# Two transformer layers on one core: all eight PSUM banks become one pool

## The chip, the core and the metric

The program runs on one core of a Trainium2 chip. The core has a tensor engine (TensorE, PE in the profile; its weight loads are the row PEld), a scalar engine (ScalarE, ACT), a vector engine (VectorE, DVE), GpSimd (POOL) and a queue that starts transfers (SyncE, SP). Each engine works through its own list of instructions in order and waits on semaphores for the others. Matmuls write into PSUM, here an array of 8 banks of 512 float32 values in each of 128 partitions; ScalarE and VectorE read them from there. The metric is the device time in microseconds (us); smaller is better.

## The reference

The input is 2048 tokens by 512 features. Four blocks run one after the other, each added to its input: attention, a mixer with an MLP, attention again, a mixer with an MLP again. The weights are the same both times.

```
def _A_ref(x, wq, wk, wv, wo):                 # x is the layer norm of the input
    q = (x @ wq).reshape(B, S, H, Dh)          # 32 heads of 16, one shared k and v
    k = x @ wk
    v = x @ wv
    scores = jnp.einsum("bhqd,bkd->bhqk", q, k) * (Dh ** -0.5)
    p = _softmax(scores, axis=-1)
    o = jnp.einsum("bhqk,bkd->bhqd", p, v)
    return o.reshape(B, S, H * Dh) @ wo

def _B_ref(x, w1, w2, w3, w4):
    h = _gelu(_layernorm(x) @ w1)              # then shift its four quarters by +-1, +-2 tokens
    x1 = x + shifted(h) @ w2
    return x1 + _gelu(_layernorm(x1) @ w3) @ w4
```

With 32 heads of only 16 features over 2048 keys, most of the work is the scores' exponentials: 32 x 2048 x 2048 of them in each layer.

## The kernel before, in words

**Tiling.** A layer's queries are cut into chunks (`CHUNKS`, line 539 on): four of 512 tokens in layer 0, three of 512 and two of 256 in layer 1. In a chunk, a block is four heads, and there are eight blocks. A block goes over 16 tiles of 128 keys, in two halves of two heads each. One such half is a *unit* of scores: for 512 queries a matmul of 32 rows for each of two heads into a bank of 512 values each (`qk`, line 1083). There are 2048 units. In the chunks of 256 queries a unit takes two key tiles at once. Chunk 0 of layer 1 is worked on while layer 0's last work still delivers keys; its blocks are cut into segments whose sums are spilled and taken up again (`make_groups`).

**Two ways for a unit.** `declare_unit` (line 1111) sends a unit to ScalarE: two banks of scores, then one exponential over both (line 1127) into one of eight buffers EA. `declare_pair` (line 1133) sends a unit to VectorE instead: each head's scores go to one bank, VectorE turns them into the bits of a coarse exponential (line 1145), and a shift by integer addition (line 1182, GpSimd, or VectorE where GpSimd has much to do) makes the two further terms that refine it. Such a unit has three terms against one in the product with the values. `assign` decides how many units go this way: it is asked when a unit's score matmuls are placed (`attach`) and looks at the free banks, VectorE's queue and the pairs in flight.

**Values.** `declare_pv` (line 1232) multiplies each term by the values and the ones beside them, 256 columns in four column tiles, and adds them up in the accumulator bank. `block_end` evicts the accumulator with VectorE (lines 1244, 1250, 1264 or 1268), sends the sums by DMA to OT, and has the softmax's denominators gathered, inverted and multiplied in.

**Side work.** Projections, mixer, MLP and norms of finished chunks run in between: their matmuls (line 676, in halves that share a bank) take a bank and VectorE evicts it. All matmuls of this kind, and filler matmuls of zeros (`filler`) that keep the tensor engine active, are placed where the attention leaves room.

**Banks.** Banks 0 to 3 belong to ScalarE's units, which take pairs 0-1 and 2-3 in turn. Bank 4 is the accumulator of every block, one after the other. Banks 5, 6 and 7 are a pool: a `Late` object stands for a bank that is chosen when the first matmul into it is placed (`take`) and goes back when its reader has been placed (`give`).

```
ACT_SLOTS = (0, 2)
ACC = 4
POOL_BANKS = (5, 6, 7)
```

When the last unit has been placed, `pump` lends the other five banks to the pool (`lend`).

**Order.** `Plan` is a planner that runs while the program is built. It steps through time with a cost for every operation and puts each engine's instructions into a fixed order. `_pick` (line 204) chooses for an engine among the operations that are ready: by priority (scores of units 0, scores of VectorE's halves 0.5, values 2, second halves of projections CLOSE, side work 10), with exceptions. For the tensor engine it knows that a change between the scores' row tiles ("Q") and the others' column tiles ("P") costs SWITCH; VectorE's scores wait for a run of scores that is going anyway (`deferred`); side work must end before the next unit's scores are due (`limits`, `due`). `TEMPER` holds a letter for each 12.5 us of planned time; it picks one of sixteen settings (`MOODS`) of nine of the planner's rules.

## Time and profile before

| | |
|---|---|
| median of 3 runs | 1471.91 us (1471.07 to 1472.3) |
| profiled execution | 1472.13 us |
| its span | 1470.2 us |
| granted clock of TensorE | 1.00 |
| TensorE busy | 1446.2 us, 98% |
| ScalarE busy | 1406.4 us, 96% |
| VectorE busy | 1295.5 us, 88% |
| GpSimd busy | 1140.3 us, 78% |
| units on ScalarE / on VectorE | 1406 / 642 |
| HBM traffic | 7.90 MB read, 2.10 MB written |

The times come from one profiled execution. A group's row gives line, engine, operation, output and input by name and shape, its count, then its busy time and the mean of one in nanoseconds, then the idle time of the engine just before, and what ended it. A row of waits gives the waiting engine and line, what it waited for, the total in us, how many times, and the longest. Ends of matmuls are modelled, so that a busy tensor engine may still be waiting inside. In the chain that ended last each piece is a start, a length and what ran.

### The profile page before, as it was taken

The page shows a single profiled execution, that of the slowest core. Times are in us where ns is not written, and L with a number is a line of the kernel's source. Part 1 is how long each engine was busy: PE and PEld are TensorE (multiplying, and loading weights), DVE is VectorE, ACT ScalarE, POOL GpSimd, SP SyncE. Part 2 cuts the span into 40 slices and gives each one's busy share as a digit, 9 for nine tenths or more (in the row PEclk, how much of TensorE's full clock was granted, in tenths as well). Part 3 has the DMA queues.
Part 4 walks back from the last instruction along what each step waited for, and adds up shares of the span by engine and source line. Part 5 has one row for each costly group of instructions (what it writes and reads, how often), then busy time and mean ns, then how long its engine had stood idle before and what let it go on. Part 6 is the DMA issues. An engine that isn't in the chain of part 4 may idle for free.

```text
span 1470.2 us, 65395 instructions
## 1 busy us (share of the span) xinstructions
PE 1446.2 (98%) x29813; PEld 646.8 (44%) x29813; DVE 1295.5 (88%) x2323; ACT 1406.4 (96%) x1496; POOL 1140.3 (78%) x830
## 2 busy tenths in 40 slices
PE   9999999999999999999999999999999999999999
PEld 4344334444443444444444444444433344555565
DVE  8899999989999889998987899999989998889873
ACT  7999999999999999999979999999999999999962
POOL 2888887878898778899854789789769968788951
PEclk9999999999999999999999999999999999999999
DMA  6100100001000000100000000010000000000000
GB/s 217 31 6 6 20 5 7 6 5 20 6 6 5 6 4 6 21 6 2 3 3 3 3 10 10 6 21 5 9 18 8 4 6 8 20 15 7 8 15 24
DMA packets 32662, 21.76 MB, mean 15 GB/s; under 512 B 13056, under 2 KB 31872, under 8 KB 32384
## 3 DMA queue, kind: packets, MB, share of 16 engines
q1 hardware_dynamic: 32384, 17.57, 5.2%
q8 instruction: 233, 3.82, 1.1%
q14 instruction: 45, 0.37, 0.1%
HBM read 7.90 MB, written 2.10 MB: 7 GB/s over the span
## 4 chain that ended last, share of the span: by engine, by line
ACT 73%; PE 22%; DVE 3%; POOL 2%; issue 0%; POOLq 0%
ACT EA L1127 68%; PE PB L676 8%; PE PB L1083 6%; PE PB L1232 6%; ACT G L1615 2%; POOL J L1182 1%; ACT L1127 1%; DVE J L1145 1%; ACT GP L1535 1%; PE PB L876 1%; ACT L1535 1%; ACT L1615 1%; DVE G L1610 0%; PE PB L933 0%; DVE J L1182 0%
## 5 line engine op out<-in xcount | busy, mean ns | idle before, releaser
L1127 ACT ACTIVATE EA<-PB 128x1024 bf16<-128x1024 f32 x1406 | 1292.9, 1172 | 12.3 <-PE PB L1083 6.1
L1182 POOL TENSOR_SCALAR J<-J 128x2048 uint16<-128x2048 uint16 (+1 forms) x534 | 976.6, 1829 | 213.9 <-DVE J L1182 90.1
L1145 DVE TENSOR_SCALAR J<-PB 128x512 uint16<-128x512 f32 x1284 | 821.8, 681 | 81.6 <-PE PB L1083 77.5
L1083 PE MATMUL PB<-QT,KT 32*128 32x512 bf16 (+1 forms) x4608 | 603.0, 360 | 11.7 <-ACT EA L1127 5.0
L1232 PE MATMUL PB<-J,VD 128*32 128x256 bf16 (+1 forms) x8628 | 418.5, 265 | 3.0 <-POOL J L1182 1.1
L1232 PE MATMUL PB<-EA,VP 128*32 128x256 bf16 (+1 forms) x6340 | 343.8, 263 | 1.0 <-DVE QT L1244 0.3
L1083 PEld LDWEIGHTS PB<-QT,KT 32*128 32x128 bf16 x4608 | 162.6, 91 | 383.6 <-ACT EA L1127 313.1
L1232 PEld LDWEIGHTS PB<-J,VD 128*32 128x32 bf16 x8628 | 179.0, 95 | 180.5 <-issue 131.1
L1232 PEld LDWEIGHTS PB<-EA,VP 128*32 128x32 bf16 x6340 | 147.6, 95 | 111.1 <-issue 91.0
L676 PE MATMUL PB<-ZT,W 128*32 128x512 bf16 (+2 forms) x2816 | 168.7, 342 | 0.6 <-DVE ZT L885 0.3
L1182 DVE TENSOR_SCALAR J<-J 128x2048 uint16<-128x2048 uint16 (+1 forms) x136 | 98.6, 725 | 7.2 <-POOL J L1182 6.5
L676 PE MATMUL PB<-W,G 128*32 128x512 bf16 x1624 | 103.5, 380 | 0.0
L1610 DVE CAST G<-PB 128x512 bf16<-128x512 f32 (+2 forms) x126 | 72.2, 581 | 11.4 <-PE PB L676 8.7
L676 PEld LDWEIGHTS PB<-ZT,W 128*32 128x32 bf16 x2816 | 63.8, 96 | 33.4 <-issue 19.3
L812 POOL TENSOR_TENSOR SM<-SM,MH 128x2 f32<-128x2 f32 (+1 forms) x69 | 50.7, 735 | 22.0 <-DVE SM L814 13.3
L1615 ACT ACTIVATE G<-G 128x1792 bf16<-128x1792 bf16 x29 | 47.0, 1686 | 19.5 <-DVE G L1610 19.4
L676 PEld LDWEIGHTS PB<-W,G 128*32 128x32 bf16 x1624 | 38.0, 96 | 37.8 <-issue 11.0
L676 PE MATMUL PB<-ONES,NIL 128*32 128x512 bf16 x532 | 49.2, 407 | 1.4 <-DVE ZT L885 0.4
L792 DVE BATCH_NORM_STATS2 ST<-X 128x6 f32<-128x512 bf16 x64 | 42.9, 678 | 1.6 <-DMA X<-in_A_x_dram 1.3
L1591 POOL TENSOR_TENSOR X<-Y,X 128x512 bf16<-128x512 bf16 x32 | 39.0, 1225 | 6.8 <-DVE Y L1573 5.9
L1268 DVE CAST ACCF<-PB 128x512 bf16<-128x512 f32 (+1 forms) x65 | 40.1, 616 | 3.7 <-PE PB L1232 3.4
L814 POOL TENSOR_SCALAR SM<-MV 128x2 f32<-128x2 f32 (+1 forms) x45 | 12.3, 272 | 31.6 <-DVE MV L794 29.7
(108 smaller groups left out, 767.3 us busy)
## 6 DMA issues: line engine op xcount, KB each, us to landing
OT<-ACCF SPq DMA_DIRECT2D x432, 8.0 KB, 1.8
W<-in_B_w_dram SPq DMA_DIRECT2D x2, 1792.0 KB, 15.0
X<-in_A_x_dram SPq DMA_DIRECT2D x8, 256.0 KB, 5.0
QT<-QS SPq DMA_DIRECT2D x32, 64.0 KB, 2.4
out_dram<-OUTB SPq DMA_DIRECT2D x16, 128.0 KB, 1.7
OT<-ACCF SPq DMA_DIRECT2D x112, 4.0 KB, 2.2
W<-in_B_w_dram SPq DMA_DIRECT2D x2, 512.0 KB, 9.8
WQ<-in_A_wq_dram SPq DMA_DIRECT2D x1, 512.0 KB, 4.6
```

The costliest lines, as they stand in the source:

```text
L676: ins = e.matmul(self.PB[32 * g:32 * g + 32, bank, 0:n], lhsT=lhsT[:, 32 * g:32 * g + 32], rhs=rhs, start=start, stop=stop, tile_position= ...
L792: op("DVE", lambda e, tb=tb: e.bn_stats(self.ST6[:, tb, :], src(tb)), reads=[tagf(tb)], writes=[("ST", tb)], dur=0.606, prio=prio)
L812: op("POOL", lambda e: e.tensor_tensor(out=out, in0=src, in1=self.MH[:, 0, a:b], op=ALU.pow), reads=tags + [("MH",)], writes=tg(r), dur=0. ...
L1083: ins = e.matmul(self.PB[:, bank, j * n:(j + 1) * n], lhsT=self.KT[32 * h:32 * h + 32, la, (kb + j) * 128:(kb + j + 1) * 128], rhs=self.QT ...
L1127: o = q.feeds = op("ACT", lambda e: e.activation(self.EA[:, ea, :, :], self.PB[:, b0:b0 + 2, :], ACTF.Exp, scale=0.25), writes=bk + [("EA" ...
L1145: o = op("DVE", lambda e, i=i, L=L: e.tensor_scalar(out=self.J[:, 3 * s, i * 512:(i + 1) * 512], in0=self.PB[:, L.bank, :], scalar1=128 * ...
L1182: o = self.pl.op(eng, lambda e: e.tensor_scalar(out=self.J[:, d, :], in0=self.J[:, f, :], scalar1=float(self.STEP), scalar2=1.0, op0=ALU.a ...
L1232: ins = e.matmul(self.PB[32 * x:32 * x + 32, self.ACC, p * hw:p * hw + hw], lhsT=v[:, la, kb + j, :], rhs=ap[:, i, j * w + u * hw:j * w + ...
L1268: self.last_copy = op("DVE", lambda e: e.tensor_copy(acc, self.PB[:, self.ACC, 0:n]), writes=[("AC",)] + am, dur=t_ps(n), prio=0, side=False)
L1591: op("POOL", lambda e, tb=tb: e.tensor_tensor(out=self.X[:, tb, :], in0=self.Y[:, tb % 6, :], in1=self.X[:, tb, :], op=ALU.add), reads=[(" ...
L1610: op("DVE", lambda e, f=f, L=L: e.tensor_copy(self.G2[:, f, 0:n], self.PB[:, L.bank, 0:n]), writes=[L] + [(x, f, i) for x in ("G2", "GE") ...
L1615: op("ACT", lambda e, i=i: e.activation(self.G2[:, :, i * 128:(i + 1) * 128], self.G2[:, :, i * 128:(i + 1) * 128], ACTF.Gelu_apprx_tanh), ...
```

## The change

Every bank is in the pool. A unit for ScalarE takes two neighbouring banks when its score matmuls are placed, and gives them back after its exponential. An accumulator is a bank of the pool too, taken at a block's first value matmul and given back at the eviction, so that the next block can begin in another bank.

Who may take what is decided in `_pick`. `coming` lists the units whose exponentials are next, with the latest start of their score matmuls (`d`), the time from which a couple of neighbours is free for them (`at`), and whether they are urgent (within LEAD and the change of mode of `d`). A unit that is not urgent is placed only where a run of scores is going and LEFT banks remain (JOIN is its priority then). `couple` picks two neighbours, 0-1 or 2-3 before others. `single` picks one bank, 4 to 7 before others, and refuses one that would leave the next unit without a couple by its time, if that is within HORIZON; units, value matmuls and fillers are not refused. `limits`, `due` and `lend` go.

Beside this, a pair for VectorE may be started with one free bank at hand (FREE 1 for 2), CLOSE is 1.9 for 2.5 and so lies below the values' priority of 2, the planner's cost of the denominators' matmuls is 60 columns for 100, the tensor engine's first matmul (which cleared bank 4) goes, and TEMPER has other letters. Other evictions are changed like the one that is shown.

```diff
-    CLOSE = 2.5
+    CLOSE = 1.9
...
+    LEAD = 0.4
+    JOIN = 0.7
+    LEFT = 1
+    HORIZON = 1.0
...
-        limit = self.limits(t) if eng == "PE" and not dense else ()
+        coming = self.coming(t) if eng == "PE" and h else ()
+        limit = [max(d, at) + self.SLACK for q, d, at, urgent in coming[:1] if at < 1e8] if not dense else ()
         joins = eng == "PE" and t < self.pe_end - 1e-9
         low = self.deferred(h, t, joins) if eng == "PE" and not dense else {}
-        pressing = joins and any(o.prio == 0 and o.ready <= t + 1e-9 for o in h) and self.pe_kind != "Q"
+        pressing = joins and self.pe_kind != "Q" and any(urgent and at <= t + 1e-9 for q, d, at, urgent in coming)
+        nfree = sum(1 for x, b in self.pool if x + self.LAT["PE"] <= t + 1e-9)
+        by = None
+        if coming and not self.loose and coming[0][1] < t + self.HORIZON and coming[0][2] < 1e8:
+            by = max(coming[0][1], t)
         stick = eng == "PE" and not dense and not joins and self.STICK is not None and t < self.pe_end + 0.05 \
             and self.pe_kind == "P" \
             and not any((0 < o.prio <= self.RUSHED if o.side else self.closing) and o.ready <= t + 1e-9 for o in h)
-        due = list(limit) + self.due(h, t) if stick else ()
+        due = limit if stick else ()
...
+            if o.feeds is not None:
+                urgent = next((x[3] for x in coming if x[0] is o), None)
+                if urgent is None:
+                    continue
+                if not urgent:
+                    if not (self.pe_kind == "Q" and t < self.pe_end + 0.05) or nfree - 2 < self.LEFT:
+                        continue
+                    key = (self.JOIN, o.seq)
...
-                k = sorted(i for i in range(len(self.pool)) if self.pool[i][0] + margin <= t + 1e-9)
-                k = sorted(sorted(k, key=lambda i: self.pool[i][0])[:o.take.n])
-                if len(k) < o.take.n or o.prio > 2 and len(self.pool) <= self.SPARE and self.attach is not None and not self.loose:
+                k = self.couple(t, margin) if o.take.n > 1 else \
+                    self.single(t, margin, None if o.feeds is not None or o.prio in (2, -20) else by)
+                if k is None:
...
+    def free_banks(self):
+        f = [1e9] * 8
+        for x, b in self.pool:
+            f[b] = x
+        return f
+    def single(self, t, margin, by):
+        f = self.free_banks()
+        best = None
+        for b in range(8):
+            if f[b] + margin <= t + 1e-9:
+                if by is not None:
+                    g = f[:b] + [1e9] + f[b + 1:]
+                    if min(max(g[i], g[i + 1]) for i in range(7)) + self.LAT["PE"] > by + 1e-9:
+                        continue
+                key = (b < 4, f[b], b)
+                if best is None or key < best:
+                    best = key
+        return None if best is None else (best[2],)
+    def couple(self, t, margin):
+        f = self.free_banks()
+        best = min(((b not in (0, 2), max(f[b], f[b + 1]), b) for b in range(7)
+                    if max(f[b], f[b + 1]) + margin <= t + 1e-9), default=None)
+        return None if best is None else (best[2], best[2] + 1)
+    def coming(self, t):
         x = max(t, self.free_at["ACT"])
+        f = self.free_banks()
+        rate = 2400.0 if self.warm else 1200.0
         res = []
+        wake = 1e9
+        for u in self.units[-6:]:
+            if u.placed:
+                continue
+            begin = x
+            x += u.dur
+            q = u.qop
+            if q.placed:
+                continue
+            if q.npend > 0 or q.ready > t + 1e-9:
+                break
+            d = begin - q.pe[1] / rate - 0.17 - self.LAT["ACT"]
+            urge = d - (self.SWITCH if self.pe_kind != "Q" else 0.0) - self.LEAD
+            at, b = min((max(f[i], f[i + 1]), i) for i in range(7))
+            if at < 1e9:
+                f[b] = f[b + 1] = 1e9
+                at += self.LAT["PE"]
+            if not all(p.placed and (p.end <= t + 1e-9 or p.eng == "PE") for p in q.take.gates):
+                at = 1e9
+            res.append((q, d, at, urge <= t + 1e-9))
+            if urge > t + 1e-9:
+                wake = min(wake, urge)
+        if wake < 1e8 and wake != self.wake:
+            heapq.heappush(self.events, wake)
+            self.wake = wake
         return res
...
-    ACT_SLOTS = (0, 2)
-    ACC = 4
-    POOL_BANKS = (5, 6, 7)
+    POOL_BANKS = range(8)
...
-    FREE = 2
+    FREE = 1
...
-    TEMPER = "090e357fe7f4ff7e0f7e2eeeff72790e3f75e5ff7145fe87e4c1e43707f90000548fe5eeef9f07ece7eeeff1f0ef9fefee4f897fe741eccccccccc"
+    TEMPER = "208e7eefffe77fe507e6ef78efe97f0913ee777f07f89ee62e7f7e6e380883840307f905e057101e3ffe544f7e03f77eef60f45335ccccccccccc"
...
-        op("PE", lambda e: e.matmul(self.PB[:, self.ACC, :], lhsT=self.NIL, rhs=self.ONES, start=True, stop=True),
-           reads=[("ONES",)], writes=[("ACC0",)], pe=mm(512), prio=-30)
...
-        if self.main_done or dep is not None and not (dep.placed and dep.end + self.pl.MARGIN <= self.pl.now):
+        if self.main_done or not (self.opener is not None and self.opener.placed) or dep is not None and not (dep.placed and dep.end + self.pl.MARGIN <= self.pl.now):
...
-            "PE", lambda e: self.dot(e, self.ACC if L is None else L.bank, 512, self.NIL, self.ONES,
+            "PE", lambda e: self.dot(e, (L or A).bank, 512, self.NIL, self.ONES,
...
-        b0 = self.ACT_SLOTS[k % 2]
+        L = Late(2)
         ea = k % self.N_EA
         hs = (2 * g[5], 2 * g[5] + 1)
 
         def fpe(e):
             ins = None
             for j, h in enumerate(hs):
-                ins = self.qk(e, g, h, b0 + j)
+                ins = self.qk(e, g, h, L.bank[j])
             return ins
-        bk = [("BK", b0), ("BK", b0 + 1)]
-        q = op("PE", fpe, reads=self.inputs(g), writes=bk, pe=("Q", 512, 256, hs), prio=0, side=False)
-        o = q.feeds = op("ACT", lambda e: e.activation(self.EA[:, ea, :, :], self.PB[:, b0:b0 + 2, :], ACTF.Exp,
-                                                       scale=0.25),
-                         writes=bk + [("EA", ea)], dur=0.06 + 1024 / 1200, prio=0, side=False)
+        q = op("PE", fpe, reads=self.inputs(g), writes=[L], pe=("Q", 512, 256, hs), prio=0, side=False, take=L)
+        o = q.feeds = op("ACT", lambda e: e.activation(self.EA[:, ea, :, :],
+                                                       self.PB[:, L.bank[0]:L.bank[0] + 2, :],
+                                                       ACTF.Exp, scale=0.25),
+                         writes=[L, ("EA", ea)], dur=0.06 + 1024 / 1200, prio=0, side=False, give=L)
+        o.qop = q
...
+        ac = ("AC", g[6] % 64)
+        if first:
+            self.acc = Late()
+        A = self.acc
...
-        op("PE", fpe, reads=rd + ([] if first else [("AC",)]), writes=[("AC",)] if first else [],
-           pe=("P", 256, 256, range(4)), prio=2, side=False)
+        o = op("PE", fpe, reads=rd + ([] if first else [ac]), writes=[ac] if first else [],
+               pe=("P", 256, 256, range(4)), prio=2, side=False, take=A if first else None)
+        if first:
+            self.opener = o
...
-            self.last_copy = op("DVE", lambda e: e.tensor_copy(acc, self.PB[:, self.ACC, 0:n]),
-               writes=[("AC",)] + am, dur=t_ps(n), prio=0, side=False)
+            self.last_copy = op("DVE", lambda e: e.tensor_copy(acc, self.PB[:, A.bank, 0:n]),
+               writes=[ac] + am, dur=t_ps(n), prio=0, side=False, give=A)
...
-        op("PE", fz, reads=am + [("SELC",)], writes=[L], pe=("P", 100 * nq, 4 * nq, range(4)), prio=fin, take=L)
+        op("PE", fz, reads=am + [("SELC",)], writes=[L], pe=("P", 60 * nq, 4 * nq, range(4)), prio=fin, take=L)
...
-            for k, o in enumerate(self.units[-2:]):
-                b0 = self.ACT_SLOTS[(self.nunit - 2 + k) % 2]
-                self.pl.lend([b0, b0 + 1], o)
-            self.pl.lend([self.ACC], self.last_copy)
```

## The prediction

> **What bounds the kernel now.** I read the page first (busy shares, then the costliest groups), then the chain that ended last, then busy times by stage, then the waits, and last two stretches of the timeline.

> ```profile
> span 1470.2 us, 65395 instructions
> ...
> PE 1446.2 (98%) x29813; PEld 646.8 (44%) x29813; DVE 1295.5 (88%) x2323; ACT 1406.4 (96%) x1496; POOL 1140.3 (78%) x830
> ...
> L1127 ACT ACTIVATE EA<-PB 128x1024 bf16<-128x1024 f32 x1406 | 1292.9, 1172 | 12.3 <-PE PB L1083 6.1
> L1182 POOL TENSOR_SCALAR J<-J 128x2048 uint16<-128x2048 uint16 (+1 forms) x534 | 976.6, 1829 | 213.9 <-DVE J L1182 90.1
> L1145 DVE TENSOR_SCALAR J<-PB 128x512 uint16<-128x512 f32 x1284 | 821.8, 681 | 81.6 <-PE PB L1083 77.5
> ```

> The attention has 2048 score units (128 keys by 512 queries by two heads). 1406 are exponentiated by ScalarE, one instruction each; the other 642 (1284 halves of 0.681 us) by VectorE, with help from GpSimd. In the chain, the second line below says 209 exponentials in 191.67 us: 0.917 us a unit, back to back.

> ```profile
> 35.91 191.67 ACT EA L1127 x209
> ...
> 605.90 97.27 ACT EA L1127 x106
> ...
> 768.45 3.93 PE PB L676 x96
> ...
> 1442.91 24.42 PE PB L676 x504
> ```

> By stage (columns: the window, its length, then busy time and count for PE, PEld, DVE, ACT, POOL, then granted clock):

> ```profile
> 50.00:750.00 700.00, 692.48 (x12944) 290.71 (x12940) 635.97 (x1101) 699.58 (x745) 586.25 (x405) 1.00 0.05 8
> 750.00:800.00 50.00, 49.63 (x1039) 23.72 (x1031) 38.73 (x83) 40.26 (x41) 19.88 (x21) 1.00 0.01 3
> 800.00:1400.00 600.00, 590.72 (x13222) 269.38 (x13220) 540.27 (x947) 598.35 (x637) 492.33 (x343) 1.00 0.05 10
> 1400.00:1470.00 70.00, 67.28 (x1732) 42.43 (x1720) 37.52 (x80) 28.75 (x37) 20.57 (x30) 1.00 0.06 20
> ```

> In the two long stages (1300 of 1470 us) ScalarE is never free: 0.42 and 1.65 us of idle time. Between the layers (750 to 800) and in the tail the tensor engine is the chain and ScalarE is short of work. So there are two ways to a shorter run: give units from ScalarE to VectorE in the long stages, or free tensor time in the two short ones. VectorE is idle 64.0 us of the 700 and 59.7 of the 600. The waits tell how much of that is scores that come late:

> ```profile
> DVE J L1145 <- PE PB L1083: 33.5, 74, 1.4
> ...
> DVE J L1145 <- PE PB L1083: 35.5, 76, 2.6
> ```

> The first is the stage 50 to 750, the second 800 to 1400: 69.0 us in 150 waits, 0.46 us each. The last view is the weight loads' waits over the whole run:

> ```profile
> PEld PB L1083 <- ACT EA L1127: 313.1, 1082, 0.8
> PEld PB L1232 <- issue: 222.1, 970, 0.8
> ...
> PEld PB L676 <- DVE J L1145: 12.1, 49, 0.5
> PEld PB L1083 <- DVE J L1145: 10.1, 38, 0.5
> ```

> 1082 times the score matmuls of a unit stand at the head of the tensor queue, 0.29 us each, until the exponential two units earlier has let its banks go. In the timeline most of that lies under the matmuls before them, which are still running.

> **The change part by part.** The sum is made against the profiled execution, 1472.13 us (span 1470.2 and 1.9 around it), 0.2 above the median of 1471.91.

> *Score units lose their own banks.* Before, four of eight banks belong to them for good and three are the pool. After, a unit becomes urgent when its exponential is nearer than the sum of the kernel's own constants: 0.213 for the matmuls, 0.17 and 0.045 of latency, 0.103 for the change of mode, LEAD 0.4: 0.93 us. That is one exponential ahead (0.917), the same moment at which a fixed slot came free before. A pair is then held for 0.93 + 0.917 = 1.85 us in every 0.917: 2.01 pairs, or 4.0 banks. If the matmuls go at the last allowed moment, 0.43 us ahead, it is 1.35 / 0.917 = 1.47 pairs, 2.9 banks. With one accumulator the pool's other users have 3.0 to 4.1 banks where they had 3. The timeline shows tensor runs of 0.3 to 0.6 us ahead of the score matmuls, so a unit seldom goes at either end; the middle is half a bank more. Units are also no longer tied to one pair, and score matmuls may go early where a run of scores is going and three banks are free.

> *What the banks buy.* A unit that moves to VectorE costs it 2 x 0.681 + 98.6/642 (its share of the shifts that VectorE does itself) = 1.516 us and saves ScalarE 0.917. The run gets shorter by that 0.917, and VectorE loses as much room: 2.43 us of VectorE's idle time a unit. Ends: none of the 69.0 us of waits is for banks, 0 us; or all are, 69.0/2.43 = 28.4 units, 26.0 us. The rows lie between: the mean wait of 0.46 us is half of a 0.917 us cycle, which is what a half waits that has just missed a score run, even with a bank free; and the pool's contention that shows openly on the tensor queue (12.1 + 10.1 us) is small because the order was planned around it. I take half: 34.5/2.43 = 14.2 units, **-13.0 us**. FREE 1 for 2 (one free bank suffices to start a pair on VectorE) is part of this.

> *What those 14 units need elsewhere.* GpSimd: 14 x 1.9 = 27 us of 330 idle. TensorE: two more value terms each; in the timeline a run of 8 value matmuls has 0.40 and one of 4 has 0.29, so 0.11 us a term, 3.1 us in all, plus 13.0 us less room. Cover: the 532 filler matmuls, 49.2 us, and the 313.1 us above. Cost 0; if the cover were gone, the 3.1 us would come on the path between the layers, where TensorE has 0.4 us left of 50.

> *One accumulator bank per block.* 86 evictions (65 of line 1268, 7 each of 1244, 1250 and 1264). Before, the next block's value matmuls wait for the eviction: 4.7 us of weight loads over 17 waits, 0.2 us of TensorE itself. That goes, but nothing on ScalarE waited for it: 0. The price is a second bank for about 0.7 us of eviction and as much of queue, 86 x 1.4 = 120 bank-us of 1370 x 8, 1%. Between 0 and a bank's worth of the above; taken as 0.

> *Head.* Until the first scores all eight banks now serve the norms and projections; the first matmul (line 738, 0.6 us) is dropped. ScalarE waits for scores 4.7 us of the first 50, but the chain there is TensorE and VectorE work, so I take 0 and keep 0 to -4.7.

> *Between the layers and tail.* More banks give no tensor time: 49.63 of 50 us are busy. Bounds 0 to half of ScalarE's 9.7 idle, -4.9; taken 0. In the tail all banks were already lent to the pool; 0.

> *Orders and costs.* CLOSE 1.9 puts second halves of projections ahead of the value matmuls (priority 2), so that their banks come free sooner: in the 13.0. The cost of the row sums' matmuls (60 for 100) and the new TEMPER letters change the order alone; the letters' mean settings hardly differ (pairs in flight 2.58 to 2.46, KEEP 0.552 both). No row prices an order; it may cost as well as gain, and ScalarE's table loads (1.28 us each, 14 at line 1127) bound it at some three to either side, +-4. Taken 0. No DMA is moved; those that follow a block's end move with it.

> *New waits.* The score matmuls of a unit now wait for whoever used the two banks last, ScalarE or VectorE or both. Behind them in the tensor queue stand value matmuls and projections, and ScalarE itself. The row of such waits on VectorE has 0.27 us each (10.1/38); there is 0.215 us of latency and up to 0.4 of LEAD above them. Taken 0; the rival below prices it.

> *The clock.* Granted is 1.00 in every window. [...]

> Sum: 1472.1 - 13.0 = **1459**.

> **The rivals.**
> 1. *Whole gain.* All waits for scores were waits for banks: 1472.1 - 26.0 = 1446; with the head and half of the layer change 1436.5. For it: VectorE is the only engine with idle time in the long stages that ends on scores. Against: the half-cycle mean.
> 2. *No change.* Bank-time stays at 4.0 because the planner places units as soon as they are urgent; VectorE keeps its 642 units: 1472, within 3. For it: the sum of the constants is the old slot's cycle.
> 3. *Slower: the slack of the score units goes.* Now ScalarE's waits in the long stages are below 2.1 us, since a fixed slot is never taken by others. If accumulators and side work split the pool so that no two neighbours are free, or the scores stand behind a tensor run, each miss costs the run one value group, 0.28 us. The gain is spent at 13.0/0.28 = 46 misses of some 1390; 100 misses make 1459 + 28 = 1487 and, with the lower half of the gain, 1493. Against: single users may not take a bank that would break the next unit's pair, and the pair just released is always two neighbours.

> **How the numbers follow.** About 0.2% (3 us) is what a measurement of this kernel can tell from no change. Chances: the forecast (1449 to 1469) 0.43; the whole gain (below 1449) 0.21; no change (1469 to 1475) 0.09; slower 0.27. So faster 0.64, same 0.09, slower 0.27. The likeliest case's own range is 1449 to 1469. The range runs from 1437 (all bounds of rival 1) to 1487 (rival 3 at 100 misses), leaving out about 0.03 below and 0.12 above.

> **What would show it.** Right: exponentials fall from 1406 to about 1392 and VectorE's halves rise from 1284 to about 1312; its wait for scores in the long stages falls from 69 to about 35 us; ScalarE stays within 3 us of full there; the weight loads' waits for the exponential fall well below 313 us, with waits for VectorE's halves above 10. Wrong: ScalarE's waits for scores above 15 us (rival 3); 642 units as before (rival 2); a granted clock below 1.00; or a longer stage between the layers, where a tensor engine with more value terms is the chain.

## The result

The change made the kernel slower: 1479.91 us (median of 7 runs, 1474.42 to 1480.88) against 1472.06 us before (1471.07 to 1472.36, 7 runs beside them). The ratio is 1.0049 with a 95% interval of 1.0039 to 1.0059. The prediction was 1459. The profiled execution of after took 1479.91 us.

From the page of after (its header, its busy row and four groups; after "|" come busy us, mean ns of one, idle time before and what ended it):

```profile
span 1478.1 us, 65127 instructions
...
PE 1446.3 (98%) x29652; PEld 640.1 (43%) x29652; DVE 1302.1 (88%) x2330; ACT 1406.0 (95%) x1494; POOL 1143.8 (77%) x835
...
L1168 ACT ACTIVATE EA<-PB 128x1024 bf16<-128x1024 f32 x1404 | 1292.4, 1168 | 23.5 <-PE PB L1125 22.6
...
L1188 DVE TENSOR_SCALAR J<-PB 128x512 uint16<-128x512 f32 x1288 | 827.6, 681 | 80.3 <-PE PB L1125 75.1
...
L719 PE MATMUL PB<-ONES,NIL 128*32 128x512 bf16 x348 | 32.0, 414 | 3.5 <-DVE WQ L772 1.7
```

ScalarE has 1404 exponentials where it had 1406, so only two units moved to VectorE, not 14. Its idle time ahead of exponentials rose from 12.3 to 23.5 us. The last row is the filler matmuls of zeros: 348, which is 87 groups of four, where before had 532 (133 groups):

```profile
L676 PE MATMUL PB<-ONES,NIL 128*32 128x512 bf16 x532 | 49.2, 407 | 1.4 <-DVE ZT L885 0.4
```

The stages (window, length, then PE, PEld, DVE, ACT and POOL busy with counts, then the granted clock) show where ScalarE lost the time:

```profile
50.00:750.00 700.00, 689.00 (x12806) 287.76 (x12805) 642.48 (x1112) 693.61 (x739) 574.36 (x397) 0.99 0.05 8
750.00:900.00 150.00, 145.53 (x2828) 64.92 (x2826) 120.59 (x229) 139.14 (x145) 95.81 (x73) 0.99 0.02 5
900.00:1400.00 500.00, 491.47 (x11182) 223.28 (x11178) 453.59 (x787) 497.41 (x529) 425.93 (x301) 0.99 0.05 10
```

In the first long stage ScalarE is idle 6.39 us (700 less 693.61); before it was 0.42. In the other two windows it is 10.86 and 2.59; the same windows of before have 140.20 and 498.41 busy, so 9.80 and 1.59 idle. And the clock is no longer 1.00.

An account of the 7.9 us, worked out from both traces: between its first and last exponential ScalarE is idle 23.6 us (before 15.9), which is +7.7; the exponentials' busy time goes from 1292.9 to 1292.4, -0.5 (two fewer should be 2 x 0.917 = -1.8, so the others take 1.3 us longer in all); after the last exponential there are 61.9 us (before 60.9), +1.0; the first one starts 0.4 us earlier, -0.4. That is 7.8 of the 7.9.

**The clock.** In the trace of after it is halved in four stretches, 24 us in all: 213.2 to 220.0, 346.3 to 353.1, 854.9 to 858.3 and 1158.7 to 1165.5. The first of them and what comes before it:

```profile
206.40:209.80 3.40, 3.40 (x83) 1.74 (x71) 3.40 (x7) 3.40 (x5) 2.91 (x7) 1.00 0.05 10
209.80:213.20 3.40, 2.32 (x37) 0.72 (x30) 1.25 (x3) 3.19 (x4) 3.22 (x3) 1.00 0.00 0
213.20:220.00 6.80, 6.80 (x100) 2.67 (x100) 5.28 (x9) 5.09 (x6) 6.46 (x6) 0.50 0.01 2
```

The stretch ahead has 37 matmuls, the one before it 83; then the clock is 0.50 for 6.8 us, and ScalarE, which depends on scores, is idle 1.71 us of them. Counted in columns (each matmul weighted with the share of the array that its tile takes, spread over its recorded time, and set against the planner's 2400 columns per us; in this trace most groups of four 512-column matmuls of the side work start 0.215 or 0.216 us before the next group), the matmuls ahead of the four falls fill 0.28, 0.34, 0.34 and 0.29 of their 3.4 us. The sparsest stretches that did not lead to a fall, on the raster of 3.413 us that each trace's own clock changes lie on (in after the halved stretches last 3.413 or 6.827 us, and the full ones between them 37, 147 and 88 times 3.413), have 0.36 and 0.38 in after and 0.40 in before. Over all kernels it is no sharp line: in after_equal2 the clock fell after 0.38, and in before_cut a stretch of 0.34 kept it.

The seven runs of after agree with that. Four with a mean clock of 0.992 took 1479.91 to 1480.88 us; those with 0.994, 0.997 and 0.999 took 1479.61, 1476.44 and 1474.42. That is about 0.30 us for each us at half the clock, and about 1473.5 at the full clock: some 6 of the 7.9 us come with the clock, some 1.5 do not, and at the full clock there is no gain either.

**What makes a stretch sparse.** Before has no gap above 0.65 us between matmuls from 50 to 1400. After has 1.02 at 211.5 and 1.35 at 344.8, each ahead of a fall, 0.91 at 852 and 0.66 at 1157 likewise, and 1.28 at 538.2 without one. At 211.5 the tensor queue stands behind a GpSimd shift that comes late (it ends at 212.5). At 344.8 it is this (timeline of after; start, length, what ran, and in brackets the idle time before with what ended it):

```profile
344.02 2.09 DVE L870 TENSOR_SCALAR ZR<-X,MV,SM 128x512 bf16<-128x512 bf16 x1
344.07 1.90 POOL L1225 TENSOR_SCALAR J<-J 128x2048 uint16<-128x2048 uint16 x1
...
346.16 0.52 PE L917 MATMUL PB<-IDENT,ZR 128*32 128x128 bf16 x16 [1.35 <-DVE ZR L870]
347.48 2.11 ACT L1168 ACTIVATE EA<-PB 128x1024 bf16<-128x1024 f32 x2 [1.27 <-PE PB L1125]
```

A norm's last step on VectorE, 0.41 us in the median of the 54 of this trace that no GpSimd shift overlaps, takes 2.09 us beside a shift that GpSimd started 0.05 us later. The transposes that need it head the tensor queue and wait; the next scores stand behind them; ScalarE has none for 1.27 us. The 42 such steps that a shift overlaps have a median of 0.81 us. What slows them, and which of the two engines issued first, can't be read from these rows.

### The profile page after: what moved, and what is told of

Read it like the earlier page. It is cut to its first block, busy times and chain, and to the rows that moved or that the text cites. A ratio compares the mean times of both kernels' runs of the same rounds, so it can differ in the third digit from the quotient of the medians.

```text
span 1478.1 us, 65127 instructions
## 1 busy us (share of the span) xinstructions
PE 1446.3 (98%) x29652; PEld 640.1 (43%) x29652; DVE 1302.1 (88%) x2330; ACT 1406.0 (95%) x1494; POOL 1143.8 (77%) x835
## 4 chain that ended last, share of the span: by engine, by line
ACT 63%; PE 26%; DVE 5%; POOL 4%; issue 1%; DMA 0%; POOLq 0%
ACT EA L1168 59%; PE PB L719 8%; PE PB L1125 8%; PE PB L1279 7%; POOL J L1225 3%; ACT G L1662 2%; DVE J L1188 2%; ACT L1168 1%; PE PB L917 1%; DVE ST L833 1%; POOL SM L853 1%; ACT GP L1582 1%; PE PB L974 0%; ACT L1582 0%; ACT L1662 0%
## 5 line engine op out<-in xcount | busy, mean ns | idle before, releaser
L1168 ACT ACTIVATE EA<-PB 128x1024 bf16<-128x1024 f32 x1404 | 1292.4, 1168 | 23.5 <-PE PB L1125 22.6
L1188 DVE TENSOR_SCALAR J<-PB 128x512 uint16<-128x512 f32 x1288 | 827.6, 681 | 80.3 <-PE PB L1125 75.1
L1279 PE MATMUL PB<-J,VD 128*32 128x256 bf16 (+1 forms) x8664 | 410.8, 265 | 5.0 <-POOL J L1225 2.4
L1279 PE MATMUL PB<-EA,VP 128*32 128x256 bf16 (+1 forms) x6328 | 357.2, 266 | 0.9 <-DVE J L1188 0.8
L1125 PEld LDWEIGHTS PB<-QT,KT 32*128 32x128 bf16 x4608 | 163.0, 91 | 391.9 <-ACT EA L1168 302.9
L1279 PEld LDWEIGHTS PB<-J,VD 128*32 128x32 bf16 x8664 | 189.1, 96 | 135.9 <-issue 87.5
L719 PE MATMUL PB<-ZT,W 128*32 128x512 bf16 (+2 forms) x2816 | 173.1, 342 | 0.4 <-DVE ZT L926 0.3
L719 PE MATMUL PB<-WO,OT 128*32 128x512 bf16 x512 | 38.6, 382 | 0.0
L719 PE MATMUL PB<-ONES,NIL 128*32 128x512 bf16 x348 | 32.0, 414 | 3.5 <-DVE WQ L772 1.7
```

Of the source, the lines that this page charges most:

```text
L719: ins = e.matmul(self.PB[32 * g:32 * g + 32, bank, 0:n], lhsT=lhsT[:, 32 * g:32 * g + 32], rhs=rhs, start=start, stop=stop, tile_position= ...
L1125: ins = e.matmul(self.PB[:, bank, j * n:(j + 1) * n], lhsT=self.KT[32 * h:32 * h + 32, la, (kb + j) * 128:(kb + j + 1) * 128], rhs=self.QT ...
L1168: o = q.feeds = op("ACT", lambda e: e.activation(self.EA[:, ea, :, :], self.PB[:, L.bank[0]:L.bank[0] + 2, :], ACTF.Exp, scale=0.25), writ ...
L1188: o = op("DVE", lambda e, i=i, L=L: e.tensor_scalar(out=self.J[:, 3 * s, i * 512:(i + 1) * 512], in0=self.PB[:, L.bank, :], scalar1=128 * ...
L1279: ins = e.matmul(self.PB[32 * x:32 * x + 32, A.bank, p * hw:p * hw + hw], lhsT=v[:, la, kb + j, :], rhs=ap[:, i, j * w + u * hw:j * w + u ...
```

## The experiments

Six kernels keep the order of one of the two and change one thing in it, or two. The others change a rule of the planner, and with it the whole order; there TEMPER's letters were chosen anew for every kernel by one and the same short search, so that no order had more care than another (only the last kernel's search was longer).

**Filler matmuls in after.** In front of the value matmuls in sparse stretches, 33 more matmuls of zeros of 512 columns (in groups of four); 17 in a second kernel, with PAD at 0.42.

```diff
+    PAD = 0.45
...
+                lack = self.PAD - act[w] / (self.WINDOW * 2400.0)
+                for o in sorted(vals.get(w, ()), key=lambda o: o.pad):
+                    if lack <= 0 or not 150.0 < o.start < 1400.0:
+                        break
+                    o.pad += 1
...
+            for _ in range(o.pad):
+                self.dot(e, A.bank, 512, self.NIL, self.ONES, False, False)
```

> The changed kernel's own order, operation for operation, with 33 more zero matmuls of 4 x 512 columns laid in front of value matmuls in the stretches of 3.4 us that hold the least matmul work (the trace of after shows the clock halved for 24 us in four places, each after such a stretch). Theory A, the clock: the seven runs of after give 1480.5 at a mean clock of 0.992, 1476.4 at 0.997 and 1474.4 at 0.999, a slope of 0.30 us per us of halved clock and 1473.5 at full clock; so clock 1.00 and 1472 to 1476, the 33 matmuls of 0.22 us costing at most 2 of it. Rival B, the order itself (scores placed late, two more value terms): the clock's drops are a consequence of a tensor engine that waits, and the time stays at 1478 to 1482, or is worse by the 7 us that the added matmuls take.

> The same with 17 added zero matmuls, only in the very sparsest stretches. Theory A: most of the four drops go, clock at or above 0.998 and 1473 to 1477; the added tensor work is half of that in the other run, so if it costs anything on the path this one is faster at equal clock. Rival B: 1478 to 1482 as after.

Measured: 1479.8 us (ratio 1.0045, 1.0033 to 1.0057) and 1479.44 (1.005, 1.0033 to 1.0066). In the trace of the first the falls at 213.2 and 346.3 stay, and so do the gaps of 1.35 us at 344.8 and 1.29 at 538.5: the added zeros stand in the same ordered queue and did not fill them. But the clock varies from run to run, and the one run at 1.00 of each took 1475.82 and 1475.11 us. So zeros alone didn't hold the clock where the queue stalled, and without falls this order takes about 1475, not less than before.

**Fewer fillers in before.** 77 groups between 200 and 1400 us have 16 columns instead of 512.

```diff
-            "PE", lambda e: self.dot(e, self.ACC if L is None else L.bank, 512, self.NIL, self.ONES,
-                                     L is not None, L is not None),
+            "PE", lambda e: self.dot(e, self.ACC if L is None else L.bank, 16 if 200.0 < o.start < 1400.0 else 512,
+                                     self.NIL, self.ONES[:, 0:16 if 200.0 < o.start < 1400.0 else 512], L is not None, L is not None),
```

> The kernel before in its own order, with its 77 zero matmuls between 200 and 1400 us cut from 512 to 16 columns (after has 35 there). Theory A: the clock falls as it does in after or more often, 0.97 to 0.995, and the time rises by 0.30 us per us of halved clock: 1476 to 1490. Rival B, fillers keep nothing up and only fill gaps: clock 1.00 and 1471 to 1473.

Measured: 1484.42 us, ratio 1.0088 (1.0071 to 1.0105). The stages:

```profile
50.00:750.00 700.00, 687.92 (x12793) 290.16 (x12796) 627.77 (x1086) 692.38 (x735) 579.08 (x397) 0.98 0.05 8
...
800.00:1400.00 600.00, 587.80 (x12818) 266.52 (x12813) 532.23 (x936) 591.17 (x627) 483.48 (x338) 0.97 0.05 10
```

Nothing but zeros is gone, the same order runs at 0.98 and 0.97, and ScalarE is idle 7.62 us in the first stage and 8.83 in the second (before 0.42 and 1.65). So before's fillers hold its clock, and fewer of them cost 12.5 us. The profiled execution was one of the slowest, 1489.12 us: its clock is halved for 58 us in seven stretches, 0.30 times that is 17.4, and it is 17.2 us above before. Here no queue stalls: the tensor engine's longest gap from 50 to 1400 is 0.64 us. The clock fell without such a stall.

**The late norms in after.** 42 of GpSimd's shifts wait until the VectorE norm or shift beside them has ended; as the change is written, they wait only for the instruction ahead of it, so that both start together.

```diff
             if x is not None and x.port and x.start <= t < x.start + self.RACE and len(self.order["DVE"]) > 1:
-                o.preds.add(self.order["DVE"][-2])
+                o.preds.add(x)
```

> The changed kernel's own order; 42 GpSimd shifts that are planned within 0.4 us after the start of a VectorE norm or shift now wait for the end of that VectorE instruction (before they waited for the one ahead of it, so that both engines started together). In the trace of after, VectorE's norm instruction of line 870 takes 2.09 us at 344.0 and at 536.7, where its mean is 0.6, each beside a GpSimd shift of 1.90 us that began 50 ns later; the transposes behind them held the tensor engine 1.35 and 1.28 us, ScalarE 1.27 and 1.10 us, and at 346.3 the clock fell. Theory C, lost races between the two engines make the long tensor stalls: both stalls go, the clock's fall at 346 goes, ScalarE's idle time of 50 to 1400 us falls by 3 to 4 of 19.9 us and the median is 1475 to 1478. Rival D, the stalls come from the new order's late scores and move elsewhere: 1479 to 1482.

> Both edits, the waits for VectorE and the 33 added zero matmuls. If the slow runs of after are stalls plus the clock that falls after them, and the zero matmuls alone failed because a stalled tensor engine issues no zero matmuls either, then together they hold the clock at 0.998 or more in most runs and give 1473 to 1476. If the order is at fault as a whole, 1479 to 1482.

Measured: 1479.18 us alone (ratio 1.0048, 1.0034 to 1.0062), 1475.84 with the 33 fillers (1.0029, 1.002 to 1.0038, 11 runs). The same norm in the timeline of the first:

```profile
344.76 0.41 DVE L870 TENSOR_SCALAR ZR<-X,MV,SM 128x512 bf16<-128x512 bf16 x1
345.26 1.90 POOL L1225 TENSOR_SCALAR J<-J 128x2048 uint16<-128x2048 uint16 x1 [0.54 <-DVE ZR L870]
345.48 0.41 PE L917 MATMUL PB<-IDENT,ZR 128*32 128x128 bf16 x16
```

Both stalls of 1.3 us are gone, and the fall at 346 with them; falls at 213.8, 852.1 and 1159.3 stay. So the first kernel's expected 1475 to 1478 was missed. With the fillers too, the first stage is almost as full as before's:

```profile
50.00:750.00 700.00, 690.45 (x12981) 288.77 (x12981) 643.43 (x1122) 698.75 (x743) 573.53 (x401) 1.00 0.05 8
```

ScalarE's idle time is 17.1 us in all (after 23.6, before 15.9). The two together give back 4.1 of the 7.9 us, and the clock is 0.999 or 1.00 in seven of the eleven runs. The five at 1.00 took 1474.69 to 1475.83, their median 3.1 us above the 1472.14 of before beside them; part of that may be the price of the added waits, for which the next experiment gives a size.

**The same wait in before** (27 shifts; the same line is changed).

> The kernel before in its own order; the 27 GpSimd shifts that are planned within 0.4 us after the start of a VectorE norm or shift now wait for the end of that instruction. In the trace of before, 15 norm instructions of line 829 and 12 shifts of line 1182 take over 0.9 us on VectorE beside a GpSimd shift, yet the longest gap of the tensor engine is 0.65 us and ScalarE is idle 2.1 us in the long stages. Theory C (a lost race costs only where the tensor engine and ScalarE have no slack behind it): 1471 to 1473, no change, since here ScalarE had nothing to win. Rival: each avoided race frees VectorE's time for the order as a whole: 1467 to 1470.

Measured: 1473.24 us, ratio 1.001 (1.0001 to 1.0019). The waits cost some 1.5 us where there is no such stall to remove, little more than can be told from nothing; they are no rule that before had missed.

**The change apart from the letters.** Both kernels with letters from the same short search (the pool here always includes FREE 1, CLOSE 1.9 and the 60 columns; no run takes them apart), and a third with the pool in which a filler may also go while only score matmuls that are not urgent are ready; as the change is written, `idle` counts those as work.

```diff
         near = self.NEAR_FILL if short < self.URGENT else 0.0
-        return not any(o.prio <= 2 and o.ready <= t + near for o in self.heap["PE"])
+        near_q = {x[0] for x in self.coming(t) if x[3]}
+        return not any(o.prio <= 2 and o.ready <= t + near and (o.feeds is None or o in near_q) for o in self.heap["PE"])
```

> The kernel before with other letters in TEMPER: all of its letters chosen anew, one after the other, by one and the same short search (for each 12.5 us the letter after which the planned progress is best over the next 62.5 us, four random continuations each) that the next two kernels also get, so that no scheme of banks has the longer search behind it. It has 1422 exponentials on ScalarE where the kernel before has 1406: 16 x 0.917 = 15 us more, so 1486 to 1502.

> The changed kernel with letters from the same search. Theory E, the pool of eight is worth about what was forecast and the kernel before only had the better letters: 5 to 15 us below the previous kernel on the same chip, with some of it lost to the clock (0.99 to 1.00). Rival F, the scheme of banks is worth nothing: it also has 1422 exponentials, so within 3 us of the previous kernel.

> The changed kernel with one line of the planner altered, and letters from the same search: a unit's score matmuls that are ready but not yet urgent no longer count as work that forbids a zero matmul (before the change a unit was not ready until its slot came free, so this case did not arise). Theory A': zero matmuls come back (146 against 129 in the previous kernel, 87 in after), the clock stays at 0.999 or above, and with 1416 exponentials it is 5 us or more below the previous kernel. Rival: the rule is idle, clock and time as in the previous kernel within 3 us.

The three again, with letters from a second draw of the search:

> A second draw for the kernel before: the same search for letters with other random continuations, two for each letter. 1420 exponentials against 1422 in the first draw: 1493 to 1503.

> The second draw for the changed kernel. Theory E, the pool is worth time under equal search: 4 us or more below the kernel ahead of it in this list, although it has 1425 exponentials against 1420 (115 groups of zero matmuls, so the clock may cost some of it). Theory H, the first comparison was luck: within 3 us of it or above.

> The second draw for the changed kernel with the idle rule, 1420 exponentials and 150 groups of zero matmuls. Theory A', the idle rule helps whatever the letters: 4 us or more below the kernel ahead of it, by 5 exponentials (4.6 us) and by less waiting of ScalarE for scores. Theory H: within 3 us of it.

Measured, with the exponentials and ScalarE's idle time between the first and the last of them:

| | first draw, us | exponentials, idle | second draw, us | exponentials, idle |
|---|---|---|---|---|
| before | 1498.20 (1.0182) | 1422, 26.6 | 1503.82 (1.0215) | 1420, 33.8 |
| after | 1492.63 (1.0145) | 1422, 20.6 | 1493.86 (1.0147) | 1425, 23.0 |
| after, idle rule | 1483.04 (1.0083) | 1416, 15.1 | 1491.87 (1.0134) | 1420, 25.7 |

The ratios are to before as it was given; each interval reaches some 0.002 to either side. So with letters of equal care the pool is worth 5.6 and 10.0 us, and the order before came with is worth more than 25 us over one with such letters. Two draws are few: those of before differ by 5.6 us between themselves, though both of after lie below both of before. The gain does not come from units: the exponentials are equal or five more. It is ScalarE's idle time, 6.0 and 10.8 us less; in the second draw much of it lies between the layers. The window from 750 to 900, before and after, second draw, one fence each:

```profile
750.00:900.00 150.00, 147.43 (x2990) 69.54 (x2990) 128.54 (x247) 128.81 (x130) 96.94 (x75) 1.00 0.02 5
```

```profile
750.00:900.00 150.00, 147.30 (x2910) 66.96 (x2902) 125.17 (x238) 136.30 (x140) 89.33 (x68) 1.00 0.02 5
```

With nearly the same tensor time ScalarE does 7.5 us more there; in the first draw it is 1.5 us there and 3.6 from 900 to 1400. The idle rule gave 9.6 us in one draw and 2.0 in the other, less than the 4 expected; whether it helps in general is left open.

**One bank fewer** (idle rule, POOL_BANKS of seven, letters by the same search).

```diff
-    POOL_BANKS = range(8)
+    POOL_BANKS = range(7)
```

> The changed kernel with the idle rule, a pool of banks 0 to 6 alone, and letters from the same search as the three kernels of equal search. What is one bank worth? Theory E (banks decide how many units VectorE can take): it has 1494 exponentials where the kernel with eight banks has 1416, 78 x 0.917 = 72 us more, so 1550 to 1570; ScalarE has next to no idle time in the long stages, and VectorE far more than before. Rival G (VectorE's waits for scores are waits for the next run of score matmuls, not for a bank): a few units move, 1483 to 1495.

Measured: 1572.36 us (two runs; ratio 1.0684, 1.0663 to 1.0705), 1494 exponentials. VectorE's waits for scores, first with eight banks (first draw, idle rule), then with seven:

```profile
DVE J L1189 <- PE PB L1126: 77.9, 168, 1.9
```

```profile
DVE J L1189 <- PE PB L1126: 195.8, 367, 1.8
```

The eighth bank is worth 89 us here (a few of them by the clock, 0.993 and 0.999 in the two runs), and its lack does show as late scores on VectorE. So such waits can be waits for banks; those that are left at eight are not shown to be.

**Score runs of VectorE's own.** ALONE is the priority of a VectorE half's score matmuls while no run of scores is going. At 11 they come after values (2) and side work (10); at 0.5 they keep their own priority, ahead of both (idle rule, letters by the same search). If a half waits because it has just missed a run, it can now start one, as long as the run ends before the next unit's scores are due.

```diff
-    ALONE = 11
+    ALONE = 0.5
```

> The changed kernel with the idle rule, eight banks, letters from the same search, and ALONE 0.5 for 11: the scores of VectorE's halves no longer wait for a run of scores that is going for a unit of ScalarE, they may start one of their own. Theory G: VectorE's waits for scores (77.9 us in the kernel of equal search with the idle rule) fall to 50 or less, while the number of score runs rises above one for each exponential and the tensor engine pays 0.23 us for each change of mode; so the time does not fall: 1483 to 1500. Theory E alone, the waits are for banks: they stay at 70 to 85 us.

Measured: 1495.12 us, ratio 1.0158 (1.0141 to 1.0175), 12.1 us above the kernel with ALONE 11. VectorE's waits:

```profile
DVE J L1189 <- PE PB L1126: 83.4, 170, 2.0
```

They are no fewer. There are 1443 score runs (1412 exponentials), against 1411 (1416) of the kernel with ALONE 11: a run of one's own was seldom started. Whether the halves lacked a bank, or the time before the next unit's scores, isn't told. The test is a weak one, since the whole order changed too; it gives the missed run no support. The expectation's price for a change of mode is too high: in this trace a group of four value matmuls starts 0.109 us after the one before it, and a score matmul 0.215 us after the last such group (medians), so a change adds some 0.11 us. The 0.23 us that the timelines show there is idle time of the weight loads.

**All together:** pool, idle rule, the shifts' wait, and letters from a longer search.

> The changed kernel with the idle rule, the waits of GpSimd for VectorE, and the best letters that a longer search of the same kind gave: 1413 exponentials (after 1404, the kernel of equal search with the idle rule 1416) and 133 groups of zero matmuls. Clock 0.999 or above; 3 x 0.917 = 3 us less than the kernel of equal search with the idle rule by the exponentials, and some more where the races are gone: 1474 to 1481. Below 1470 it would beat both kernels; that would need ScalarE as full as in before with nine exponentials more than after, so it isn't expected.

Measured: 1485.13 us, ratio 1.009 (1.0074 to 1.0105), 1413 exponentials, 18.1 us of idle time. It is below the first draw's 1492.63 for the pool as it is, and above both kernels as given and the expected 1474 to 1481. No kernel that was run beats before.

## Why the prediction was wrong

**"What the banks buy" (-13.0 us): the step that failed first.** It had 14.2 units move to VectorE, and two did. VectorE's waits for scores over the whole run went from 77.5 to 75.1 us only. In the long stages they are:

```profile
DVE J L1188 <- PE PB L1125: 32.3, 70, 2.2
...
DVE J L1188 <- PE PB L1125: 36.2, 69, 2.3
```

The first row is 50 to 750, the second 800 to 1400. Against 50 to 750 of before they should be read with care: the prediction's row of 33.5 us in 74 waits covers 100 to 750, not 50 to 750 as it says; the longer window has 38.6 us in 84. So the waits fell from 74.1 to 68.5, not to 35. The argument by which half of them were waits for banks and the other half for a run just missed, a mean of half a cycle, has no support: own_score_runs let the halves start runs, 32 more came, and the waits stayed. What the 75 us are waits for is open. Open too is why a bank more bought no units here, when seven_banks prices the eighth at 78. `assign` also stops at the pairs in flight and at VectorE's queue, and the new letters lower the first limit (mean 2.58 to 2.46, which the prediction passed over); no run varies it by itself.

**"Score units lose their own banks": about right.** A unit's score matmuls go some 0.49 us (median, after; 0.50 before) ahead of its exponential, so a pair is in use (0.49 + 0.917) / 0.917 = 1.53 times over, 3.1 banks, the lower end of the estimated 2.9 to 4.0. Nearly a bank was freed. It did not buy units.

**"Between the layers" (0, bound -4.9): wrongly emptied.** "More banks give no tensor time" is right, but with equal letters 1.5 and 7.5 us of the pool's worth lay from 750 to 900. With equal letters the gain is 5.6 and 10.0 us where 13.0 was forecast, and it comes without the units that were to make it; as far as the size is near, that is luck.

**"Orders and costs" (0, +-4): the term that decided the sign.** Letters and order are not a matter of a few table loads: before as it was given is 26.1 and 31.7 us faster than before with other letters (1498.20 and 1503.82 less 1472.1), but after as it was given only 12.7 and 14.0 us faster than after with other letters (1492.63 and 1493.86 less 1479.91). Before's letters are thus worth some 13 and 18 us more to their kernel than after's are to theirs, and that outweighs the pool's 5.6 and 10.0. The clock that after's order loses is part of it. No row of before shows this, and for that reason a bound of 4 was too narrow.

**"The clock" (0): wrong by some 6 us.** The prediction read 1.00 in every window and then spent the 532 fillers as free cover, without asking what they were there for. The change itself makes them rarer: 133 groups to 87, with equal letters 178 and 171 to 129 and 115. That ready score matmuls which may wait count as work is part of the reason; the idle rule brings 146 and 150. before_cut prices such a loss by itself. The trace of after shows ahead of each fall one sparse stretch of 3.4 us with a gap of 0.66 to 1.35 us; that the use of the banks has a part in it is not shown. A fall of 6.8 us cost some 2.0 us (0.30 x 6.8).

**"New waits" (0) and the slower rival: the outcome, by another road.** That rival expected ScalarE's slack to go because two neighbouring banks would be missing. ScalarE's waits for scores are indeed above its mark of 15:

```profile
ACT EA L1168 <- PE PB L1125: 22.6, 21, 10.1
```

It is 21 waits and not 46, one of them 10.1 us between the layers. Those that were followed come from a tensor queue that stands behind a late norm or shift, or from half the clock. after_port_pad33 takes most of them out of the first stage without touching a bank. The weight loads' waits for the exponential, expected well below 313.1 us, are 302.9; those for VectorE's halves are 13.7, above 10 as stated.

**"One accumulator bank per block", "Head", "What those 14 units need elsewhere":** The weight loads' 4.7 us of waits for the eviction are gone, with no gain that can be seen on ScalarE. In the first 50 us ScalarE does 0.9 us more (40.36 against 39.48), near the 0 taken. What 14 units need was not tested, since they never moved. In the tail the time after the last exponential is 1.0 us longer, near its 0.

What stays open: where the last 1.5 to 3 us at full clock lie; how much the pool is worth exactly, with two draws at 5.6 and 10.0, and how much of it is the banks and not FREE or CLOSE; and whether it beats before under an order as good as before's, which none of the searched letters reached.

## What to carry to other kernels

Before counting filler matmuls as free room, price the clock that they hold: here 77 groups of zeros cut short cost 12.5 us. A planner's order that was tuned with its rules is a part of them, and a rule is compared fairly only under orders of equal care, or within one order. An engine's wait that looks like a lack of some resource is tested by taking one more away and by removing its rival cause, not by the mean of the wait.
